# First of equal maxima: a rank and a second maximum, or a product with a constant matrix

## The chip, the cores and the metric

The kernel runs on one core of a Trainium2 chip. A core has a matrix engine (TensorE, in the profile PE, with its weight loads as PEld), a vector engine (VectorE, DVE), a scalar engine (ScalarE, ACT), a general engine (GpSimd, POOL) and DMA queues, most of them issued from SyncE (SP). The engines run side by side, each through its own instructions in order, and wait for each other by semaphores. TensorE writes its results to PSUM; the rest of the data lies in SBUF. The metric is device time in microseconds (us) from the first to the last instruction.

## The reference, cut to what matters

Routed attention over 4 batches, 8 heads, 768 positions and 64 channels, and then a dense block on the result. Each query and each key is assigned to one of 16 clusters, and a query attends only to keys of its own cluster.

```python
q_assign = np.argmax(np.einsum('bhsd,hcd->bhsc', q_n, c_n), axis=-1)   # q_n, k_n, c_n: normed
k_assign = np.argmax(np.einsum('bhsd,hcd->bhsc', k_n, c_n), axis=-1)
mask = q_assign[:, :, :, None] == k_assign[:, :, None, :]
scores = scale * np.matmul(q, k.transpose(0, 1, 3, 2))
scores = np.where(mask, scores, -1000000000.0)
scores = scores - np.max(scores, axis=-1, keepdims=True)
attn = np.exp(scores)
attn = attn / (np.sum(attn, axis=-1, keepdims=True) + 1e-09)
x = attn @ v                       # then (B,H,S,D) -> (B*S, H*D) = 3072 x 512
h = x @ w_in                       # 512 x 2048
sp = np.maximum(h, 0.0) + np.log1p(np.exp(-np.abs(h)))
return (h * erf(sp)) @ w_out       # 2048 x 512
```

`argmax` takes the first of equal maxima. That tie rule is what the change computes in another way. The weights arrive as 64-bit floats, and the kernel turns them into 32-bit ones itself; this "conversion" is integer work on VectorE, ScalarE and GpSimd.

## The kernel before

The kernel works on pairs of heads: 4 batches of 4 pairs, 16 pairs in all. Each pair is first *routed* (every query and key gets its cluster), then *shifted* (a maximum of the masked scores per query), then its scores, exponentials and attention values are computed in 12 units (two halves of the queries by six blocks of keys). For batch 0 this is done in 48 slots, one unit each, in the order of the program text. In the first-slot work of a pair, the routing of the next pair is already carried along. From slot 45 on, the dense block is mixed in, and after slot 48 the order of the instructions is no longer kept to the program text.

The mask is carried by the product itself. Beside the 64 channels, the tiles `qm` and `km` hold 32 rows with one entry per cluster: for the query 1 at its cluster and 0 elsewhere, for the key 0 at its cluster and a huge negative number elsewhere. Their product is then 0 where the clusters agree and huge and negative where not.

The routing, cut (`P` = 128, `D` = 64, `C` = 16, `HW` = 384, `Q` = 32, `BIG` = 2^60):

```python
def route(p):
    ...
    for nm in "qk":                               # step 1: inputs
        raw = rowp.tile([P, S], F32, name=nm + "T")
        ve.transpose(out=raw, in_=st.pop(nm).rearrange("p n t -> p (n t)"))
    load_qk(p + 1)
    yield
    psim = ps_x.tile([P, HW], F32, name="psim", tag="x")
    for g in range(4):                            # step 2: similarities
        te.matmul(psim[2 * C * g : 2 * C * (g + 1)], lhsT=ccT[:, p % HP], rhs=...)
    vectors("q")                                  # ScalarE: query channels to bf16
    yield
    sims = routep.tile([P, HW], F32, name="sims") # step 3: which ones are maxima
    ve.transpose(out=sims, in_=psim)
    sim = sims.rearrange("p (g c) -> p g c", c=C)
    ve.reduce_max(out=mx, in_=sim, axis=AX.X)
    ve.tensor_tensor(out=sim, in0=sim, in1=mx..., op=ALU.is_equal)
    yield
    vectors("k")                                  # step 4: key channels to bf16
    yield
    ve.tensor_tensor(out=sim, in0=sim, in1=rank..., op=ALU.mult)        # step 5
    ve.reduce_max(out=mr, in_=sim, axis=AX.X)
    hot = routep.tile([P, HW], BF16, name="hot")
    for r, op in ((slice(0, D), ALU.is_equal), (slice(D, P), ALU.subtract)):
        ve.tensor_tensor(out=hot[r]..., in0=sim[r], in1=mr[r]..., op=op)
    hotT = routep.tile([P, HW], BF16, name="hotT")
    ve.transpose(out=hotT, in_=hot)
    yield
    ...                                           # step 6: hotT to qm and km:
    ve.tensor_scalar_mul(out=low["q"][r, e, cols], in0=hotT[g], scalar1=own[g, e : e + 1])
    ae.copy(out=low["k"][r, e, cols], in_=hotT[g])                      # 4 of these
    ae.activation(out=dst, in_=src, func=ACT.Copy, scale=scale)         # 2, after them
    yield
```

The equality gives 1 for every maximum, so two equal ones both get a 1. The product with `rank` (16 for the first cluster, down to 1 for the last, times `BIG` in the key half) and a second maximum single out the first.

Shift, scores and sums, cut to what the text speaks of:

```python
sm = ps_x.tile([P, HW], F32, name="sm", tag="x")         # 24 per pair, two per step
te.matmul(sm, lhsT=st["qm"][...], rhs=st["km"][...])
ve.tensor_reduce(out=nmx[...], in_=sm, axis=AX.X, op=ALU.max, negate=True)
...
te.matmul(sc[...], lhsT=st["kT"]..., rhs=st["qT"]...)    # scores, float part
te.matmul(sc[...], lhsT=st["km"]..., rhs=st["qm"]...)    # scores, mask and shift
ae.activation(out=pr, in_=sc, func=ACT.Exp, scale=D**-0.5)
ge.tensor_tensor(out=acc, in0=..., in1=pr, op=ALU.add)   # sums of the exponentials
te.matmul(st["av", half]..., lhsT=st["v"][:, j, e], rhs=pr)
te.matmul(psum..., lhsT=minus, rhs=acc)                  # then den on VectorE, and xT
...
hp = ps_x.tile([P, GW, TB], F32, name="hp", tag="x")     # dense block, hidden
po = ps_x.tile([P, DM], F32, name="po", tag="x")         # dense block, output
```

The pool `ps_x` has four PSUM buffers for all of psim, sm, av, psum, hp and po. Each hidden and output tile is moved out of PSUM by VectorE (`g`, `osb`), and every finished hidden chunk goes through a gate of Softplus and Erf on ScalarE and products on GpSimd.

In the 48 slots, a table says how many steps of the current pair, of the next pair (ahead of and behind the scores), and of the conversion go into each of a pair's 12 slots.

Of the kernel before, what the change touches and what calls it, by code (L numbers as in the profile page):

```python
# [23 lines left out]
HW = S // 2  # L24
# [11 lines left out]
BIG = 2.0**60  # L36
# [30 lines left out]
def kernel(  # L67
# [24 lines left out]
    routep = pool("routep", 1)  # L92
# [7 lines left out]
    ps_x = pool("ps_x", 4, space=PSUM)  # L100
# [4 lines left out]
    rank = const.tile([P, C], F32, name="rank")  # L105
# [40 lines left out]
    def load_qk(p):  # L146
        load(p, "q", q, stage)
        load(p, "k", k, stage, nc.sync if p else nc.scalar)
# [12 lines left out]
            ge.memset(t["k"][e * D + SH : e * D + SH + 1, e], 1.0)  # L161
    for t in prs:
        ge.memset(t[:, :, HW : HW + 2], EPS)

# [85 lines left out]
    for it in range(2):  # L250
# [4 lines left out]
            out=twice, in0=ss, scalar=inv, in1=norm, op0=ALU.mult, op1=ALU.add  # L255
# [3 lines left out]
            out=norm, in0=twice, scalar1=0.5, scalar2=(1e-6 if it else 0.0),  # L259
            op0=ALU.mult, op1=ALU.add,  # L260
# [11 lines left out]
    def route(p):  # L272
        st = pairs[p]
        low = lows[p % 2]
        for e in range(2 if p > 1 else 0):
            r = e * D + SH
            nc.sync.dma_start(out=low["q"][r : r + 1, e], in_=low["q"][r + 1 : r + 2, e])
        for nm in "qk":
            raw = rowp.tile([P, S], F32, name=nm + "T")
            ve.transpose(out=raw, in_=st.pop(nm).rearrange("p n t -> p (n t)"))  # L280
            st[nm + "T"], st[nm + "m"] = raw, low[nm]
# [16 lines left out]

        vectors("q")
        yield  # L300

        sims = routep.tile([P, HW], F32, name="sims")
        ve.transpose(out=sims, in_=psim)
        n = HW // C
        sim = sims.rearrange("p (g c) -> p g c", c=C)
        mx = routep.tile([P, n], F32, name="mx")
        ve.reduce_max(out=mx, in_=sim, axis=AX.X)
        ve.tensor_tensor(
            out=sim, in0=sim, in1=mx.unsqueeze(2).to_broadcast([P, n, C]), op=ALU.is_equal
        )  # L310
        yield
        vectors("k")
        yield

        ve.tensor_tensor(
            out=sim, in0=sim, in1=rank.unsqueeze(1).to_broadcast([P, n, C]), op=ALU.mult
        )
        mr = routep.tile([P, n], F32, name="mr")
        ve.reduce_max(out=mr, in_=sim, axis=AX.X)

        hot = routep.tile([P, HW], BF16, name="hot")
        for r, op in ((slice(0, D), ALU.is_equal), (slice(D, P), ALU.subtract)):
            ve.tensor_tensor(
                out=hot[r].rearrange("p (g c) -> p g c", c=C), in0=sim[r],
                in1=mr[r].unsqueeze(2).to_broadcast([D, n, C]), op=op,
            )
        hotT = routep.tile([P, HW], BF16, name="hotT")
        ve.transpose(out=hotT, in_=hot)
        yield
        late = []  # L330
        for half in range(2):
            cols = slice(half * HW, (half + 1) * HW)
            for e in range(2):
                r = slice(e * D, e * D + Q)
                g = slice(half * Q, (half + 1) * Q)
                if half == 0:
                    ve.tensor_scalar_mul(out=low["q"][r, e, cols], in0=hotT[g], scalar1=own[g, e : e + 1])
                else:
                    late.append((low["q"][r, e, cols], hotT[g], own[g, e : e + 1]))
                g = slice(D + half * Q, D + (half + 1) * Q)  # L340
                ae.copy(out=low["k"][r, e, cols], in_=hotT[g])
        for dst, src, scale in late:
            ae.activation(out=dst, in_=src, func=ACT.Copy, scale=scale)
        yield


# [249 lines left out]
    def aside(p):  # L596
# [12 lines left out]
    def advance(p, n):  # L609
        for _ in range(n):  # L610
            next(ready[p])
# [12 lines left out]
    for c in range(C):  # L624
        ve.memset(rank[0:D, c : c + 1], float(C - c))
    ve.tensor_scalar_mul(out=rank[D:P], in0=rank[0:D], scalar1=BIG)
    ve.memset(alleps, S * EPS)
    for t in maxima:
        ve.memset(t, FLOOR)
# [50 lines left out]
    for u in range(2 * NJ * HP, len(units), 2):  # L680
        p, half, j = units[u]
# [59 lines left out]
```

## Time and profile before

| | before |
|---|---|
| median of 3 runs | 1228.26 us (1228.07 to 1229.61) |
| profiled execution | span 1227.4 us, mean granted TensorE clock 0.978 |
| hidden products `hp` | 384.4 us busy, 1536 records |
| output products `po` | 367.8 us busy, 768 records |
| maxima `nmx` | 195.4 us busy on VectorE, 384 instructions |
| exponentials `pr` | 147.4 us busy on ScalarE, 192 instructions |
| HBM read, written | 35.68 MB, 6.29 MB |

A page of the profile gives for each engine its busy time and share, then the span in 40 equal slices with the busy share in tenths, then the DMA queues, the chain of waits that ended last, and the costliest groups of instructions. A group's line reads: engine, operation, output from inputs by the names in the program, shapes, count, then busy time and the mean of one in ns, then how long the engine was idle just ahead of these instructions and which engine ended most of it. One float product counts as two records, because it takes two passes. Busy times can also be asked for any stretch of time, and waits as a list of who waited for whom: total, how often, longest.

In the chain of the whole span, TensorE has 74%, VectorE 11%, ScalarE 6%, DMA 2% and GpSimd 1%; 7% is time in which an engine waited for nothing that the profile shows.

### The profile page before, as it was taken

What the parts mean: (1) busy time and instruction counts of PE and PEld (TensorE: products, weight loads), DVE (VectorE), ACT (ScalarE), POOL (GpSimd) and SP (SyncE); (2) the same over time, 40 slices, a digit from 0 to 9 for tenths busy, and PEclk for the clock granted to TensorE, in tenths of its full rate; (3) what the DMA queues carried; (4) which work ended last, traced back from release to release, by engine and by line L of the source; (5) the groups of instructions that cost most, each with busy time, mean ns of one, the idle gap of its engine ahead of it and who ended that gap; (6) DMA issues with size and microseconds to landing.
All of it is one profiled execution on the core that took longest, in us unless ns stands there. A gap on an engine that the chain in (4) does not pass through costs nothing.

```text
span 1227.4 us, 13359 instructions
## 1 busy us (share of the span) xinstructions
PE 1158.3 (94%) x4897; PEld 618.2 (50%) x4897; DVE 541.5 (44%) x999; ACT 567.8 (46%) x675; POOL 465.8 (38%) x462
## 2 busy tenths in 40 slices
PE   4888879989999999999999999999999999999998
PEld 1222235554354445555456445556456456576663
DVE  6889885675444345334344344334435112011121
ACT  3656656647362647164364445356264254032222
POOL 2467764357332345244234144235234343030200
PEclk8889999889999999999999999999999999999999
DMA  7344323132020202010020201002000000000000
GB/s 134 77 105 104 81 82 84 41 103 33 16 48 9 39 9 39 9 35 13 10 48 1 48 10 27 21 10 39 4 27 1 9 9 1 12 6 17 1 18 18
DMA packets 140753, 42.95 MB, mean 35 GB/s; under 512 B 133520, under 2 KB 133520, under 8 KB 140688
## 3 DMA queue, kind: packets, MB, share of 16 engines
q1 hardware_dynamic: 137552, 41.70, 15.2%
q10 hardware_dynamic: 3136, 0.39, 0.3%
q8 instruction: 39, 0.64, 0.2%
q14 instruction: 26, 0.21, 0.1%
HBM read 35.68 MB, written 6.29 MB: 34 GB/s over the span
## 4 chain that ended last, share of the span: by engine, by line
PE 74%; DVE 11%; issue 7%; ACT 6%; DMA 2%; POOL 1%; SPq 0%; ACTq 0%; DVEq 0%
PE po L58 25%; PE hp L58 24%; PE sc L58 12%; PE av L58 7%; PE sm L58 4%; DVE nmx L58 3%; ACT L58 2%; DVE w_out L58 2%; DVE den L58 1%; DVE sims L58 1%; ACT inv L58 1%; PE psim L58 1%; PE psum L58 1%; ACT km L58 1%; ACT pr L58 1%
## 5 line engine op out<-in xcount | busy, mean ns | idle before, releaser
L58 PE MATMUL hp<-xT,w_in 128*128 128x256 f32 x1536 | 384.4, 387 | 4.1 <-DVE xT L58 2.4
L58 PE MATMUL po<-w_out,g 128*128 128x512 f32 x768 | 367.8, 597 | 0.6 <-DVE den L58 0.6
L58 POOL TENSOR_TENSOR acc<-acc,pr 128x384 f32<-128x384 f32 x256 | 240.3, 968 | 318.0 <-ACT pr L58 317.9
L58 PEld LDWEIGHTS hp<-xT,w_in 128*128 128x128 f32 x1536 | 287.2, 192 | 124.0 <-issue 79.8
L58 DVE TENSOR_REDUCE nmx<-sm 128x1 f32<-128x384 f32 x384 | 195.4, 551 | 144.9 <-PE sm L58 144.0
L58 ACT ACT_TABLE_LOAD x113 | 145.0, 1283 | 230.7 <-DVE g L58 128.8
L58 ACT ACTIVATE pr<-sc 128x768 f32<-128x768 f32 x192 | 147.4, 807 | 166.7 <-PE sc L58 166.4
L58 PEld LDWEIGHTS po<-w_out,g 128*128 128x128 f32 x768 | 141.8, 190 | 108.0 <-issue 95.0
L58 PE MATMUL sc<-qT,kT 64*128 64x384 f32 x768 | 185.3, 537 | 6.2 <-ACT pr L58 6.1
L58 POOL TENSOR_TENSOR g<-a_s,g 128x512 f32<-128x512 f32 x88 | 110.6, 1287 | 198.4 <-ACT a_s L58 198.4
L58 DVE COPY g<-hp 128x512 f32<-128x512 f32 x96 | 65.9, 687 | 257.1 <-PE hp L58 256.8
L58 PE MATMUL av<-pr,in_v 128*64 128x386 f32 x768 | 144.5, 505 | 2.5 <-DVE nmx L58 2.5
L58 PE MATMUL sm<-km,qm 128*128 128x384 bf16 x384 | 106.1, 342 | 31.3 <-DVE nmx L58 14.5
L58 PEld LDWEIGHTS sc<-qT,kT 64*128 64x128 f32 x768 | 70.9, 190 | 85.4 <-issue 45.6
L58 POOL TENSOR_TENSOR acc<-pr,pr 128x384 f32<-128x384 f32 x64 | 66.7, 1063 | 94.2 <-ACT pr L58 94.2
L58 PEld LDWEIGHTS av<-pr,in_v 128*64 128x64 f32 x768 | 50.0, 138 | 92.8 <-issue 78.7
L58 PEld LDWEIGHTS <-qm 128*128 128x128 bf16 x384 | 35.2, 99 | 99.6 <-issue 73.2
L58 DVE SCALAR_TENSOR_TENSOR den<-psum,inv 128x384 f32<-128x384 f32 x32 | 17.8, 557 | 145.5 <-ACT inv L58 145.1
L58 ACT ACTIVATE a_s<-a_s 128x2048 f32<-128x2048 f32 (+2 forms) x40 | 55.8, 1413 | 13.3 <-DMA a_s<-in_moe_w_out_dram 8.9
L58 PE MATMUL sc<-qm,km 64*128 64x384 bf16 x384 | 59.5, 329 | 1.9 <-DMA qm<-nmT 1.9
L58 ACT ACTIVATE a_s<-g 128x2048 f32<-128x2048 f32 x24 | 45.8, 1910 | 33.0 <-DVE g L58 31.8
L58 ACT COPY nmT<-pn 6x128 bf16<-6x128 bf16 x32 | 8.1, 252 | 98.3 <-PE pn L58 97.9
(66 smaller groups left out, 604.7 us busy)
## 6 DMA issues: line engine op xcount, KB each, us to landing
w_out<-in_moe_w_in_dram SPq DMA_DIRECT2D x16, 512.0 KB, 4.5
in_q<-in_q_dram SPq DMA_DIRECT2D x64, 96.0 KB, 3.0
in_v<-in_v_dram SPq DMA_DIRECT2D x32, 192.0 KB, 3.0
out_dram<-osb SPq DMA_DIRECT2D x24, 256.0 KB, 2.0
in_k<-in_k_dram SPq DMA_DIRECT2D x60, 96.0 KB, 3.3
a_s<-in_moe_w_out_dram SPq DMA_DIRECT2D x8, 512.0 KB, 3.4
w_out<-in_moe_w_out_dram SPq DMA_DIRECT2D x8, 512.0 KB, 4.3
qm<-nmT SPq DMA_DIRECT2D x192, 0.2 KB, 1.7
```

What stands on the lines that cost most here:

```text
L58: ins = getattr(self.engine, name)(*args, **kw)
```

## The change

It is meant to take vector work out of the routing. The equality now writes `hot` at once, as bf16, with a 1 at every maximum. After the transpose, a product with a constant 128x128 bf16 matrix `first` finds the first one: `first` has 1 on its diagonal and -1 wherever its row is an earlier cluster of the same group of 16. A result is then its own hot entry minus the number of hot entries before it: 1 at the first maximum, 0 or negative everywhere else. The query half is scaled by `own` and cut off at 0 on the way out of PSUM; the key half becomes `BIG` times the result minus `BIG`, which is 0 at the first maximum and at or below `-BIG` elsewhere. The results `won` lie in a buffer of `ps_x`, where `hotT` lay in SBUF.

```diff
+    ge.memset(first, -1.0)
+    for base, pattern, sign, op, fill in (
+        (-1, [[1, P]], -1, ALU.is_ge, 0.0),
+        (0, [[-C, P // C], [0, C]], 1, ALU.is_ge, 0.0),
+        (0, [[-1, P]], 1, ALU.not_equal, 1.0),
+    ):
+        ge.affine_select(out=first, in_=first, compare_op=op, fill=fill, ...)
...
         ve.reduce_max(out=mx, in_=sim, axis=AX.X)
+        hot = routep.tile([P, HW], BF16, name="hot")
         ve.tensor_tensor(
-            out=sim, in0=sim, in1=mx.unsqueeze(2).to_broadcast([P, n, C]), op=ALU.is_equal
+            out=hot.rearrange("p (g c) -> p g c", c=C), in0=sim,
+            in1=mx.unsqueeze(2).to_broadcast([P, n, C]), op=ALU.is_equal,
         )
-        yield
-        vectors("k")
-        yield
-
-        ve.tensor_tensor(out=sim, in0=sim, in1=rank..., op=ALU.mult)
-        mr = routep.tile([P, n], F32, name="mr")
-        ve.reduce_max(out=mr, in_=sim, axis=AX.X)
-        hot = routep.tile([P, HW], BF16, name="hot")
-        for r, op in ((slice(0, D), ALU.is_equal), (slice(D, P), ALU.subtract)):
-            ve.tensor_tensor(out=hot[r]..., in0=sim[r], in1=mr[r]..., op=op)
         hotT = routep.tile([P, HW], BF16, name="hotT")
         ve.transpose(out=hotT, in_=hot)
         yield
+        won = ps_x.tile([P, HW], F32, name="won", tag="x")
+        te.matmul(won, lhsT=first, rhs=hotT, start=True, stop=True)
+        yield
         for half in range(2):
             for e in range(2):
                 if half == 0:
-                    ve.tensor_scalar_mul(out=low["q"]..., in0=hotT[g], scalar1=own[g, e : e + 1])
+                    ve.tensor_scalar(
+                        out=low["q"]..., in0=won[g], scalar1=own[g, e : e + 1], scalar2=0.0,
+                        op0=ALU.mult, op1=ALU.max,
+                    )
                 else:
-                    late.append((low["q"]..., hotT[g], own[g, e : e + 1]))
+                    ae.activation(out=low["q"]..., in_=won[g], func=ACT.Relu, scale=own[g, e : e + 1])
-                ae.copy(out=low["k"]..., in_=hotT[g])
+                ae.activation(
+                    out=low["k"]..., in_=won[g], func=ACT.Identity, bias=nbig[g], scale=BIG
+                )
-        for dst, src, scale in late:
-            ae.activation(out=dst, in_=src, func=ACT.Copy, scale=scale)
         yield
+        vectors("k")
+        yield
...
     plan = (                       # own steps, next pair's before and behind, conversion
-        (1, 0, 1, 1), (1, 0, 2, 0), (1, 0, 2, 0), (1, 0, 1, 0), (0, 0, 0, 0), (0, 0, 2, 0),
-        (0, 0, 2, 1), (0, 0, 2, 1), (0, 1, 0, 3), (0, 0, 0, 3), (0, 0, 2, 1), (0, 0, 1, 2),
+        (1, 0, 1, 0), (1, 0, 2, 0), (1, 0, 2, 1), (1, 0, 1, 0), (0, 0, 1, 2), (0, 0, 2, 0),
+        (0, 0, 1, 2), (0, 0, 1, 2), (0, 1, 0, 2), (0, 1, 0, 0), (0, 0, 2, 1), (0, 0, 1, 2),
     )
...
         if r % NJ == 2 and slot > 2:
+            if after:
+                advance(p + 1, 1)
+                after -= 1
             part = divide(slot - 3)
             next(part)
```

The order of the steps in a pair becomes: inputs; similarities; maxima, `hot` and its transpose; the product; the copies to `qm` and `km`; the key channels to bf16. It is again six steps. In the plan by slots, the two steps of maxima that stood together in slots 6 and 7 are spread over slots 4 to 9, one or two at a time, and the conversion's twelve steps lie in other slots. In the slot where a half's sums are formed, the next pair's product comes ahead of them.

More of the change, by code (lines that the diff above doesn't have):

```diff
@@ L104 @@
     minus = const.tile([P, D], F32, name="minus")
-    rank = const.tile([P, C], F32, name="rank")
+    first = const.tile([P, P], BF16, name="first")
+    nbig = const.tile([P, 1], F32, name="nbig")
     ccT = const.tile([P, HP, 2 * C], F32, name="ccT")
@@ L163 @@
         ge.memset(t[:, :, HW : HW + 2], EPS)
+    ge.memset(first, -1.0)
[4 more added lines that the diff above has]
+    ):
+        ge.affine_select(
+            out=first, in_=first, compare_op=op, fill=fill, base=base, pattern=pattern,
+            channel_multiplier=sign,
+        )
     w_steps = []
@@ L307, in route @@
         ve.reduce_max(out=mx, in_=sim, axis=AX.X)
+        hot = routep.tile([P, HW], BF16, name="hot")
         ve.tensor_tensor(
-            out=sim, in0=sim, in1=mx.unsqueeze(2).to_broadcast([P, n, C]), op=ALU.is_equal
-        )
-        yield
-        vectors("k")
-        yield
-        ve.tensor_tensor(
-            out=sim, in0=sim, in1=rank.unsqueeze(1).to_broadcast([P, n, C]), op=ALU.mult
-        )
-        mr = routep.tile([P, n], F32, name="mr")
-        ve.reduce_max(out=mr, in_=sim, axis=AX.X)
-        hot = routep.tile([P, HW], BF16, name="hot")
-        for r, op in ((slice(0, D), ALU.is_equal), (slice(D, P), ALU.subtract)):
[L323 to L326, printed above, removed]
+            out=hot.rearrange("p (g c) -> p g c", c=C), in0=sim,
+            in1=mx.unsqueeze(2).to_broadcast([P, n, C]), op=ALU.is_equal,
+        )
         hotT = routep.tile([P, HW], BF16, name="hotT")
@@ L329, in route @@
         yield
-        late = []
+        won = ps_x.tile([P, HW], F32, name="won", tag="x")
+        te.matmul(won, lhsT=first, rhs=hotT, start=True, stop=True)
+        yield
         for half in range(2):
@@ L336, in route @@
                 if half == 0:
-                    ve.tensor_scalar_mul(out=low["q"][r, e, cols], in0=hotT[g], scalar1=own[g, e : e + 1])
-                else:
-                    late.append((low["q"][r, e, cols], hotT[g], own[g, e : e + 1]))
+                    ve.tensor_scalar(
+                        out=low["q"][r, e, cols], in0=won[g], scalar1=own[g, e : e + 1], scalar2=0.0,
+                        op0=ALU.mult, op1=ALU.max,
+                    )
+                else:
+                    ae.activation(
+                        out=low["q"][r, e, cols], in_=won[g], func=ACT.Relu, scale=own[g, e : e + 1]
+                    )
                 g = slice(D + half * Q, D + (half + 1) * Q)
-                ae.copy(out=low["k"][r, e, cols], in_=hotT[g])
-        for dst, src, scale in late:
-            ae.activation(out=dst, in_=src, func=ACT.Copy, scale=scale)
+                ae.activation(
+                    out=low["k"][r, e, cols], in_=won[g], func=ACT.Identity, bias=nbig[g], scale=BIG
+                )
+        yield
+        vectors("k")
         yield
@@ L623 @@
     ve.memset(minus, -1.0)
-    for c in range(C):
-        ve.memset(rank[0:D, c : c + 1], float(C - c))
-    ve.tensor_scalar_mul(out=rank[D:P], in0=rank[0:D], scalar1=BIG)
+    ve.memset(nbig, -BIG)
     ve.memset(alleps, S * EPS)
```

## The prediction

> **What bounds the kernel now.** I read the page first: busy time by engine, then its forty slices, to see whether one engine bounds the whole span.
>
> ```profile
> span 1227.4 us, 13359 instructions
> ...
> PE 1158.3 (94%) x4897; PEld 618.2 (50%) x4897; DVE 541.5 (44%) x999; ACT 567.8 (46%) x675; POOL 465.8 (38%) x462
> ...
> PE   4888879989999999999999999999999999999998
> ...
> DVE  6889885675444345334344344334435112011121
> ```
>
> There are two regimes. One slice is 30.7 us. In the first six or seven slices (batch 0, attention with almost no dense layer beside it) TensorE is not full and VectorE is at 8 to 9 tenths. From about 194 us on, TensorE is full and VectorE is at 3 to 5 tenths. The 44% of VectorE over the whole span describes neither. So I asked for busy times by stretch: three head pairs of the first regime, each from one pair's input transposes to the next one's, and the long middle.
>
> ```profile
> 34.50:71.40 36.90, 31.45 (x145) 9.59 (x144) 29.48 (x54) 22.58 (x36) 20.56 (x20) 0.84 0.44 103
> 71.40:107.70 36.30, 31.52 (x172) 10.30 (x172) 33.15 (x60) 23.97 (x37) 25.14 (x25) 1.00 0.39 92
> 107.70:145.00 37.30, 31.99 (x161) 9.88 (x160) 32.72 (x60) 23.59 (x38) 24.84 (x25) 0.95 0.37 89
> ```
> ```profile
> 330.00:1072.00 742.00, 733.81 (x3161) 398.86 (x3159) 277.43 (x514) 337.57 (x387) 263.78 (x264) 1.00 0.10 20
> ```
>
> The columns are length, then TensorE, weight loads, VectorE, ScalarE, GpSimd. In the first regime a pair takes 36 to 37 us, of which VectorE works about 33 and TensorE about 32: two nearly full engines in program order, each waiting for the other in turn. In the middle TensorE is busy 733.8 of 742 us (99%): only its own work counts there, and 8 us is all that removing waits could bring.
>
> The waits between 34.5 and 194 us say what the gaps are:
>
> ```profile
> DVE nmx L58 <- PE sm L58: 15.5, 13, 2.7
> ```
> ```profile
> PE sm L58 <- DVE nmx L58: 9.9, 12, 2.4
> ```
>
> The first is VectorE waiting for a score product before its maximum, the second a score product waiting for a PSUM buffer that a maximum has yet to free. They come from the bursts of four maxima in one slot.
>
> Last, the groups of VectorE in the same window, for the operations that the change touches:
>
> ```profile
> L58 DVE TENSOR_TENSOR hot<-sims,mr 64x384 bf16<-64x384 f32 x8 | 7.1, 884 | 0.2
> ...
> L58 DVE TENSOR_SCALAR qm<-hotT,own 32x384 bf16<-32x384 bf16 x8 | 4.9, 618 | 0.3
> L58 DVE TENSOR_TENSOR sims<-sims,mx 128x384 f32<-128x384 f32 x4 | 3.9, 984 | 0.1
> ...
> L58 DVE TENSOR_TENSOR sims<-sims,rank 128x384 f32<-128x384 f32 x4 | 3.5, 882 | 0.0
> ...
> L58 DVE TENSOR_REDUCE mr<-sims 128x24 f32<-128x384 f32 x4 | 2.2, 553 | 0.1
> ```
>
> The last numbers before the second bar are mean ns of one. The four operations that go (rank product, second maximum, two halves of hot) lie one after another in the chain of waits of this regime, with nothing of another engine between them.
>
> [...]
>
> **The change, part by part.** There are 16 pairs: pair 0 in the prologue, pairs 1 to 4 routed in the first regime, pairs 5 to 15 in the second.
>
> *Removed from VectorE, first regime, per pair:* 0.882 + 0.553 + 2 x 0.884 = 3.20 us. The equality stays, with a bf16 output; I leave it at 0.98. The two query copies on VectorE stay, from PSUM in place of SBUF: 2 x 0.62 before; I put 0.55 for each, as the maxima from PSUM (0.548) and the first denominator step (0.554) take, so 0.1 us is gained.
>
> *Added to VectorE:* the second query copy waits for ScalarE to finish its first key copy from the same tile. A 32x384 copy of ScalarE took 0.51 us, so VectorE idles about 0.6 us per pair. Net, VectorE is relieved of about 2.7 us in a period of 36.5.
>
> *What of it reaches the end:* VectorE works some 33 of 36.5 us and TensorE 32, so relief of VectorE alone is soon stopped by TensorE. I let three quarters through: 2.0 us per pair. *Spreading the maxima* removes part of the burst waits, 15.5 us over 4.3 periods = 3.6 us each; I take a quarter, 0.9 us. *The product* costs TensorE about 0.35 us per pair here (a score product of the same shape took 0.350). Sum: 2.0 + 0.9 - 0.35 = 2.5 us per pair, times 4 = **10 us gained in the first regime**. The conversion steps are the same twelve per pair, elsewhere in the slots.
>
> *Prologue (pair 0):* the chain sims, maximum, equality, rank product, second maximum, two halves, transpose, ScalarE copies ran without a gap. It loses 0.57 + 0.56 + 1.12 = 2.25 us of VectorE and gains about 0.4 us of product. But the two key casts (0.84 us each), which were hidden under VectorE, now come after the winner copies, and these alternate between VectorE and ScalarE for about 0.5 us more: 1.7 + 0.4 + 0.5 = 2.6 us back. **About 0.**
>
> *Second regime, 11 pairs:* the VectorE relief is worth nothing, and the product is new work for the bound. Two score products of its shape took 0.49 us together at 0.33 each, so one adds 0.16 us: 11 x 0.16 = 1.8 us. Then, TensorE takes its work in order, and the product stands in its queue soon after the similarities. For pair 8, before:
>
> ```profile
> 414.65 0.49 PE L58 MATMUL psim<-kT,ccT 128*32 128x384 f32 x2
> 415.08 0.70 PE L58 MATMUL hp<-xT,w_in 128*128 128x256 f32 x2
> 415.61 1.88 PE L58 MATMUL po<-w_out,g 128*128 128x512 f32 x4
> 417.33 0.59 PE L58 MATMUL hp<-xT,w_in 128*128 128x256 f32 x2
> ```
>
> The similarities end at 415.14. VectorE begins their transpose at 415.21, and its steps start 0.6 us apart (415.21, 415.83, 416.42, 417.01), so a fourth step, the transpose of hot, would end at 417.6: 2.45 us after the similarities. A dense product is two passes of 0.215 us (hp) or 0.43 us (po), so 0.43 or 0.86 us. In the built order of the changed kernel, what stands between similarities and winners for pairs 5 to 15 is between 2.1 us (four hp, one score) and 4.5 us, mostly 2.6 (six hp, three po, or two and two) or 3.4 (eight hp, or two po and four hp). Against 2.45 us plain, or 3.1 us where a dense eviction (0.68) falls between, or over 3.5 us where GpSimd stretches the equality (1.68 us at 298.5), TensorE waits 0 to 1 us. I take 0.3 us on average: 11 x 0.3 = 3.3 us. **Second regime: 1.8 + 3.3, about 5 us lost.**
>
> Sum: -10 + 0 + 5 = -5 us. I lean a little further, because the new plan by slots looks fitted to the new step lengths: 1228.3 - 7.3 = **1221 us**.
>
> **The rivals.** *First: TensorE pays for it.* The winners stay in one of only four PSUM buffers that hidden layer, output, attention values, sums and score products also use. Eight reads that partly alternate between engines hold it 4.5 us or more; where ScalarE is inside a gate (activations of 1.9 us, table loads of 1.28 us; at 557 us its copies took until 569) it is held 8 us or longer, and the sums product after the attention values then finds no buffer. Before, the copies came out of SBUF and held none. For it: one of those waits alone is 2 to 3 us of the bound. Against: most pairs have 4 us of attention products first, which cover the hold. It would make 1228 to 1235. *Second: the first regime is set by TensorE, not VectorE.* For it: its 32 busy us per period. Against: it waits for VectorE there, and the chain runs mostly over VectorE. Then 2 us per pair at most would be spread's, and the time 1226 to 1230. *Third: both engines loosen together*, because a removed VectorE operation also frees buffers earlier and shortens TensorE's waits: 4 us per pair, 1210 to 1213.
>
> **Range and chances.** First regime 4 to 17 us gained, second 2 to 12 us lost; the two extremes seldom meet: 1211 to 1231. Faster by over 2% means under 1203.7 us, 24.6 us less: and TensorE's gaps in the three periods shown are only 5.5, 4.8 and 5.3 us, so four periods hold some 21 us: 0.03. Slower by over 2% would need more than 3 us lost in each of the eleven later pairs, on top of the gain: 0.02.
>
> **What would show it.** In the first regime the period from one pair's input transposes to the next should be about 34 us in place of 36.5, with VectorE busy near 30 and its wait for score products under 15 us; the dense layer should begin about 10 us earlier. From there to the end it should take about 5 us longer, with winners' products waiting for the hot transpose by 3 us in sum. The prediction is wrong if the first-regime period stays above 36 (rival two), or if hidden, output or sums products wait for ScalarE by more than 5 us (rival one).

## The result, and the profile after

The changed kernel takes **1242.2 us** (median of 4 runs, 1241.8 to 1245.3). Against the kernel before, timed on the same chip, the ratio is 1.0114 with a 95% interval of 1.0095 to 1.0132: slower by 1.1%, where I had predicted 1221 us and a gain.

The page of the changed kernel, the lines that answer to those shown of before:

```profile
span 1240.1 us, 13300 instructions
...
PE 1167.3 (94%) x4913; PEld 622.6 (50%) x4913; DVE 496.1 (40%) x919; ACT 567.6 (46%) x673; POOL 463.5 (37%) x466
...
PE   3788969899999999999999999999999999999998
...
DVE  5578876554434244333334244343335112011121
...
PEclk8689999989999999999999999999999999999999
```

VectorE did lose work: 541.5 us busy before, 496.1 now. In most of the first ten slices it stands a tenth or more lower, but TensorE does not stand higher there. The last line is new to this text: it is the TensorE clock that was granted, and it has dips early in the run. The kernel before had such dips too:

```profile
PEclk8889999889999999999999999999999999999999
```

To see where the time went I use one milestone in all that follows: the product that sums the exponentials of one half of a pair (`psum`). There are 32, numbered 0 to 31; number 10 is the first of pair 5, where the routing is already in the later regime. Start times in the two traces:

| sums product | before | after | later by |
|---|---|---|---|
| 0 | 56.29 | 62.80 | 6.5 |
| 10 | 335.44 | 337.32 | 1.9 |
| 17 | 559.80 | 564.22 | 4.4 |
| 18 | 596.77 | 604.89 | 8.1 |
| 31 | 1029.86 | 1042.49 | 12.6 |

So the first part (up to number 10) gained nothing and lost 1.9 us; 6.5 us are already lost at number 0, and some of that comes back. The later part lost 10.7 us, and not evenly: 3.7 us of it between numbers 17 and 18. The spans differ by 12.7 us, so this is the whole loss.

**First part.** Busy time by stretch, one pair of the first regime, from its input transposes to the next pair's (columns: length, TensorE, weight loads, VectorE, ScalarE, GpSimd, then granted clock, DMA share, GB/s):

```profile
113.50:150.00 36.50, 32.54 (x164) 10.21 (x163) 28.75 (x55) 23.53 (x36) 24.76 (x25) 0.95 0.40 90
```

VectorE works 28.7 us per pair, some 4 less than before. The period is still 36.5 us. (From input transposes to input transposes, the first three periods are 42.8, 36.5 and 36.5 us; before they were 39.0, 36.3 and 37.3. The stretch of 36.9 us that the prediction shows first begins 2.2 us behind that pair's transposes.) VectorE now waits instead: for score products, between 34.5 and 194 us, 28.8 us in all where it was 15.5:

```profile
DVE nmx L58 <- PE sm L58: 28.8, 18, 4.9
```

TensorE's waits between 14 and 200 us show two that are new in size (before: 3.2 us for the first, none for the second):

```profile
PE sm L58 <- ACT km L58: 9.8, 4, 5.9
PE pn L58 <- DVE den L58: 8.4, 3, 2.8
```

Of the first, 6.2 us belong to pair 0. The second comes once in each of three pairs. The timeline of one, cut to the instructions that hand it on (start, duration, engine, operation; in brackets what the engine had waited for):

```profile
118.74 0.34 PE L58 MATMUL won<-hotT,first 128*128 128x384 bf16 x1 [0.24 <-DVE hotT L58]
119.27 0.87 PE L58 MATMUL psum<-acc,minus 128*64 128x384 f32 x4 [0.20 <-DVE nmx L58]
119.71 0.60 DVE L58 TENSOR_SCALAR qm<-won,own 32x384 bf16<-32x384 f32 x1
...
120.24 0.58 ACT L58 ACTIVATE inv<-psum,alleps 128x384 f32<-128x384 f32 x1 [0.84 <-PE psum L58]
...
121.40 0.57 ACT L58 ACTIVATE km<-won,nbig 32x384 bf16<-32x384 f32 x1
122.01 0.61 DVE L58 TENSOR_SCALAR qm<-won,own 32x384 bf16<-32x384 f32 x1 [1.70 <-ACT km L58]
...
122.99 0.55 DVE L58 SCALAR_TENSOR_TENSOR den<-psum,inv 128x384 f32<-128x384 f32 x1
...
123.59 0.22 PE L58 MATMUL pn<-identb,nm 128*6 128x128 bf16 x1 [2.81 <-DVE den L58]
...
124.75 1.56 PE L58 MATMUL av<-pr,in_v 128*64 128x386 f32 x4
```

Read from the bottom: TensorE waits 2.81 us for a PSUM buffer, which `den` frees. `den` stands in VectorE's queue behind the second query copy, that copy waits 1.70 us for ScalarE's first key copy of the same tile `won`, and that one stands behind the two `inv` steps. All this while `won`, sums and attention values hold the four buffers. Then a second cost: after the gap the attention product takes 1.56 us where the same four records took 0.85 us at 119.94. The granted clock in the stretch behind the gap is 0.59 (the last column but two of this row; it was 1.00 in the 6 us before):

```profile
124.00:128.00 4.00, 4.00 (x16) 1.10 (x14) 0.88 (x3) 3.90 (x7) 0.00 (x0) 0.59 0.01 0
```

**Later part.** ScalarE and VectorE around sums product 17 (564.22 us after, 559.80 before), first the changed kernel, then the kernel before:

```profile
563.04 1.91 ACT L58 ACTIVATE a_s<-a_s 128x2048 f32<-128x2048 f32 x1
...
567.32 0.57 ACT L58 ACTIVATE km<-won,nbig 32x384 bf16<-32x384 f32 x1
...
569.20 0.58 ACT L58 ACTIVATE inv<-psum,alleps 128x384 f32<-128x384 f32 x1
...
572.35 0.56 DVE L58 SCALAR_TENSOR_TENSOR den<-psum,inv 128x384 f32<-128x384 f32 x1 [2.78 <-ACT inv L58]
```
```profile
562.24 0.58 ACT L58 ACTIVATE inv<-psum,alleps 128x384 f32<-128x384 f32 x1
...
565.22 0.56 DVE L58 SCALAR_TENSOR_TENSOR den<-psum,inv 128x384 f32<-128x384 f32 x1 [7.37 <-ACT inv L58]
```

Five copies out of `won` (the last is at 567.32) now stand between the gate (`a_s`) and the logarithm of the sums (`inv`). The logarithm starts 5.0 us after the sums product, against 2.4 us before, and `den` 8.1 against 5.4. TensorE then waits 1.06 us for the attention output `xT` that `den` leads to (at 574.34 us), and the granted clock falls once more (0.57 between 575 and 579 us). Number 25 shows the same: the logarithm starts 5.0 us after the sums product, against 2.4 us before. From number 10 to number 31 TensorE is idle for 11.9 us in all, against 8.2 before.

### The profile page after: what moved, and what is told of

It reads as the page before. It is cut to its first block, busy times and chain, and to the rows that moved or that the text cites. A ratio compares the mean times of both kernels' runs of the same rounds, so it can differ in the third digit from the quotient of the medians.

```text
span 1240.1 us, 13300 instructions
## 1 busy us (share of the span) xinstructions
PE 1167.3 (94%) x4913; PEld 622.6 (50%) x4913; DVE 496.1 (40%) x919; ACT 567.6 (46%) x673; POOL 463.5 (37%) x466
## 4 chain that ended last, share of the span: by engine, by line
PE 62%; ACT 7%; issue 6%; DVE 3%; DMA 1%; POOL 0%; ACTq 0%; SPq 0%; DVEq 0%; POOLq 0%
PE po L58 24%; PE hp L58 21%; PE sc L58 9%; PE av L58 5%; PE sm L58 3%; ACT L58 2%; ACT a_s L58 2%; ACT km L58 1%; ACT inv L58 1%; PE psum L58 1%; DVE den L58 1%; DMA a_s<-in_moe_w_out_dram 1%; ACT pr L58 1%; PE psim L58 1%; ACT qm L58 1%
## 5 line engine op out<-in xcount | busy, mean ns | idle before, releaser
L58 PE MATMUL hp<-xT,w_in 128*128 128x256 f32 x1536 | 389.7, 390 | 10.4 <-DVE xT L58 6.8
L58 ACT ACTIVATE a_s<-a_s 128x2048 f32<-128x2048 f32 (+2 forms) x40 | 55.8, 1412 | 16.6 <-DMA a_s<-in_moe_w_out_dram 16.4
L58 ACT ACTIVATE km<-won,nbig 32x384 bf16<-32x384 f32 x64 | 36.6, 573 | 32.1 <-DVE qm L58 31.3
```

The lines of the kernel that those rows point to most:

```text
L58: ins = getattr(self.engine, name)(*args, **kw)
```

## The experiments

The first theory was my rival one: the result of the product is held in PSUM by readers on two engines that wait for one another. Its rivals: the product itself, the new order of steps (the copies one step earlier, the casts of the key channels one step behind them in place of two steps ahead), and the new plan. All runs in one table; the last two columns are from each run's trace, in us against the kernel before (positive is later): where sums product 10 starts, and what is lost from there to number 31.

| run | median us | ratio, 95% interval | to no. 10 | 10 to 31 |
|---|---|---|---|---|
| changed kernel | 1242.2 | 1.0114 [1.0095, 1.0132] | +1.9 | +10.7 |
| e1 result moved to SBUF | 1239.3 | 1.0094 [1.0064, 1.0123] | +1.2 | +11.6 |
| e2 no product | 1234.4 | 1.0063 [1.0042, 1.0084] | -11.9 | +12.4 |
| e3 rank, new plan | 1212.7 | 0.9886 [0.9866, 0.9906] | -16.4 | 0.0 |
| e4 product, old plan | 1247.3 | 1.0179 [1.0143, 1.0215] | +9.8 | +7.5 |
| e5 casts with the product | 1241.9 | 1.0100 [1.0065, 1.0134] | +3.1 | +10.9 |
| e7 e5, result in SBUF | 1229.9 | 1.0019 [1.0005, 1.0033] | -4.7 | +8.2 |
| e8 e5, no product | 1231.6 | 1.0028 [1.0010, 1.0047] | -13.9 | +18.4 |
| e9 e3, casts late | 1235.9 | 1.0066 [1.0045, 1.0087] | +8.8 | +1.6 |
| e11 old order, SBUF | 1208.6 | 0.9839 [0.9791, 0.9887] | -24.0 | +1.2 |
| e12 old order, no product | 1215.4 | 0.9890 [0.9849, 0.9930] | -25.1 | +13.5 |
| e13 e3, old conversion | 1230.7 | 1.0026 [1.0010, 1.0043] | -0.9 | +3.3 |
| e14 old order from pair 5 | 1238.8 | 1.0103 [1.0067, 1.0138] | -5.2 | +11.1 |
| e15 e12, late transpose | 1215.7 | 0.9895 [0.9866, 0.9924] | -24.1 | +13.5 |
| e16 e11 from pair 5 | 1230.8 | 1.0023 [1.0009, 1.0037] | +0.9 | -0.4 |
| e17 e11 up to pair 4 | 1218.3 | 0.9916 [0.9889, 0.9943] | -20.7 | +10.8 |

e2, e8, e12 and e15 leave the tie rule out: every maximum stays marked. The column up to number 10 comes from single executions and moves by some us from one to another: up to sums product 5, e14 and the changed kernel run the same program, and stand at +3.7 and +7.3, with a granted clock of 8 tenths and 6 tenths in the second fortieth of the span.

**e1: the result leaves PSUM by one copy**, at the head of the next step.

```diff
         te.matmul(won, lhsT=first, rhs=hotT, start=True, stop=True)
         yield
+        wonb = routep.tile([P, HW], BF16, name="wonb")
+        ve.tensor_copy(out=wonb, in_=won)      # all eight copies then read wonb
```

> The changed kernel, but the product's result is moved to SBUF (bf16) by one VectorE copy right after it, and the eight copies read that. It adds some 0.6 us of VectorE per pair and frees the PSUM buffer at once; the reads of the two engines no longer wait for one another. Theory A (the held PSUM buffer and the alternating reads take the gain): the 2.8 us wait of the transpose of the row maxima for a buffer, once per pair in the first regime, goes, and so do the cold stretches after it; about 1229 us (1225 to 1233). Theory B (ScalarE's order, the key casts after the copies, takes it): hardly any change, 1239 to 1242. Theory C (the new plan by slots takes it): no change, 1241 to 1243. Theory D (the product's own time on the full TensorE takes it): no change.

Measured: 0.2% less in the ratio, with overlapping intervals, and next to nothing gained in either part. The move does what it is for: `won` is held 0.9 to 1.5 us per pair in place of 5.2 to 9.6, and the waits of the row maxima's transposes for `den` are gone. So the hold by itself was not the whole cause. The wait of the first score product for the key copies and casts grew to 20.6 us between 14 and 200 us (9.8 in the changed kernel): ScalarE, not the buffer, was now in the way.

**e2: no product**, the copies read `hotT` (tie rule left out), all else as changed.

```diff
-        won = ps_x.tile([P, HW], F32, name="won", tag="x")
-        te.matmul(won, lhsT=first, rhs=hotT, start=True, stop=True)
```

> The changed kernel without the product: the copies read the transposed hot tile itself, so that all of several equal maxima count (the tie rule is left out). It shows what taking away the vector operations is worth alone, with the changed plan and step order. Theory A: the lost time comes back and part of the relief shows, 1222 to 1228 us. Theory B or C: it stays at 1238 to 1242, for the casts and the plan are as in the changed kernel. Theory D: some 3 to 6 us below the changed kernel.

Measured: still slower than before by 0.6%, with four vector instructions less and nothing put in their place. The later part loses 12.4 us with no product in it. So order or plan costs by itself.

**e3: the kernel before with the new plan; e4: the changed kernel with the old plan.** Each swaps the table of slots and the early step ahead of the sums.

> The kernel before (rank and second maximum) with the new plan by slots and the step moved ahead of the sums: the plan alone. Theory C: the plan itself costs, 1236 to 1243 us. Theories A and B: within 4 us of the kernel before, and if the spread of the maxima does what it is for, 1223 to 1228.

> The changed kernel's routing with the plan by slots of the kernel before: the product alone. Theory A: the winners' copies now come after the sums, so the buffers are as short, and it stays at 1237 to 1244 us. Theory B: the first maxima come a slot later than in the new plan, so the casts are done in time: 1233 to 1238. Theory C: 1228 to 1232.

Measured: the plan alone makes the kernel before 1.1% **faster**, all of it before sums product 10, and nothing is lost later. The old plan makes the changed kernel slower still. The plan is acquitted; what remains is the order of the steps and the product.

**e13: which column of the plan.** e3 with the maxima spread as in the new plan, the conversion's twelve steps where they were.

```diff
-        (1, 0, 1, 0), (1, 0, 2, 0), (1, 0, 2, 1), (1, 0, 1, 0), (0, 0, 1, 2), (0, 0, 2, 0),
-        (0, 0, 1, 2), (0, 0, 1, 2), (0, 1, 0, 2), (0, 1, 0, 0), (0, 0, 2, 1), (0, 0, 1, 2),
+        (1, 0, 1, 1), (1, 0, 2, 0), (1, 0, 2, 0), (1, 0, 1, 0), (0, 0, 1, 0), (0, 0, 2, 0),
+        (0, 0, 1, 1), (0, 0, 1, 1), (0, 1, 0, 3), (0, 1, 0, 3), (0, 0, 2, 1), (0, 0, 1, 2),
```

> The kernel with rank and new plan, with the conversion's steps put back into the slots of the old plan: the spread of the maxima alone. If the spread is what gained 1.1%, ratio 0.987 to 0.991; if the conversion's new places gained it, 0.996 to 1.004. My guess is that the spread gives two thirds: 0.991 to 0.994.

Measured: 1.0026. Spread maxima alone gain nothing; with them in place, the conversion's new places are worth the step from 1.0026 to 0.9886, about 17 us. The new places with the old maxima were not run, so the two may need each other.

**e5, e7, e8: casts of the key channels ahead of the copies again**, in the same step as the product, e7 with the move to SBUF too, e8 without the product.

```diff
         te.matmul(won, lhsT=first, rhs=hotT, start=True, stop=True)
+        vectors("k")
         yield
...
-        vectors("k")
         yield
```

> The changed kernel with one line moved: the two key casts on ScalarE stand with the product, ahead of the winners' copies, as they did in the kernel before. Theory B (the casts behind the copies hold up the first maxima of a pair): the waits of score products for ScalarE's key tiles fall from 9.8 us (more in the kernel with the SBUF copy: 20.6) to under 4, the prologue is 1.5 to 2 us shorter, and the time is 1225 to 1232 us. Theory A (the held buffer and the alternating reads): at most 2 to 4 us less than the changed kernel, 1238 to 1240, with the 2.8 us waits of the transposes of row maxima still there.

> Both mendings at once: casts ahead of the copies, and the product's result moved to SBUF by one VectorE copy. If A and B each hold one half of the loss (the copy alone gave only 3 us because the late casts then stood in the way), it lies clearly under both single mendings: 1214 to 1224 us. If B alone matters, it equals the kernel with the early casts within 3 us. Against the kernel before it should be faster, for the plan alone gave 1.1%.

> No product (the copies read the transposed hot tile, the tie rule is left out) and the casts ahead of the copies: the vector operations taken away, with nothing put in their place. Against the kernel with the rank and the new plan (ratio 0.9886 to the kernel before) this shows what the four vector operations were worth. If VectorE bounds the first regime: 10 us or more below it, ratio 0.977 to 0.981. If latency and TensorE bound it: the same within 4 us, ratio 0.985 to 0.991.

Measured: e5 is as slow as the changed kernel: TensorE's waits for the key tile fall from 9.8 to 5.9 us, but those of the row maxima's transposes for `den` are still there (10.2 us between 14 and 200 us). e7 stands below e1 (1.0019 against 1.0094), so the place of the casts matters once the buffer is free, but it still only draws level with the kernel before. In these three, the plan's slot of two steps takes casts (1.68 us) and copies (six of 0.57 us) of ScalarE together, and a later step stands empty. So they did not test the old order cleanly. e9 and e11 come closer to it.

**e9: the old chain with the casts late**: e3, with `vectors("k")` moved behind the copies, into the same step (in the changed kernel they have a step of their own behind them).

```diff
-        vectors("k")                # step 4
         yield
...
+        vectors("k")                # step 6, behind the copies
         yield
```

> The kernel with the rank and the new plan (ratio 0.9886 to the kernel before), and only the two key casts moved behind the winners' copies. Theory B: they cost 8 to 20 us here too, ratio 0.995 to 1.005, with new waits of score products for ScalarE. Theory A: under 3 us, ratio 0.987 to 0.991.

Measured: 1.0066 against 0.9886 for e3. Moving two casts costs 1.8%, about 22 us, nearly all in the first part, with no product in the kernel: late casts can cost this much by themselves. The waits of TensorE for the key tile between 14 and 200 us, e9 first, then e3:

```profile
PE sm L58 <- ACT km L58: 27.4, 10, 6.2
```
```profile
PE sm L58 <- ACT km L58: 7.6, 6, 2.5
```

The first maxima need `km` whole: copies and casts. In e9 ScalarE does both in one stretch, 5 us long, with the next score product waiting at its end. In the changed kernel this happens in the first two pairs alone (9.8 us in sum); the later ones wait for `den`, as shown above.

**e11: the order of the kernel before, with the product and the move to SBUF.** Casts at step 4, product and move at step 5, copies at step 6.

```diff
         ve.transpose(out=hotT, in_=hot)
         yield
+        vectors("k")
+        yield
...
         te.matmul(won, lhsT=first, rhs=hotT, start=True, stop=True)
+        wonb = routep.tile([P, HW], BF16, name="wonb")
+        ve.tensor_copy(out=wonb, in_=won)
         yield
...                                 # copies from wonb
         yield
-        vectors("k")
-        yield
```

> The changed kernel with the steps of a pair in the order of the kernel before: equality and hot transpose in step 3, key casts in step 4, product and its move to SBUF in step 5, copies to qm and km in step 6. In the second regime the copies then come after the logarithm of the sums on ScalarE, as before, and not ahead of it. Theory E (the copies, made ready earlier, went ahead of the logarithm and so held the sums' and attention buffers): the steps of 4, 2 and 2 us that the changed kernel loses at pairs 10, 13 and 14 go; from the sums of pair 5 to the end it loses under 4 us against the kernel before, and the time is 1213 to 1222. Theory A or B alone: the second regime still loses 8 us or more, 1226 to 1232.

Measured: **1208.6 us, ratio 0.9839 [0.9791, 0.9887]**: faster than the kernel before and than the changed kernel, with nothing left out, and below the 1213 to 1222 that I had expected. Against e3, the rank in the same plan, the intervals overlap: that the product beats the rank is not shown. The granted clock by slices of its profiled execution (span 1204.6 us), and the stretch from 36 to 180 us, e11 first, then the changed kernel:

```profile
PEclk9999999999999999999999999999999999999999
```
```profile
36.00:180.00 144.00, 131.11 (x666) 48.33 (x663) 128.83 (x229) 96.72 (x150) 107.40 (x100) 0.99 0.43 104
```
```profile
36.00:180.00 144.00, 124.98 (x603) 38.76 (x603) 106.28 (x200) 90.53 (x140) 90.00 (x87) 0.91 0.38 88
```

In the same 144 us, e11 gets 666 matmul records done against 603, and at a clock of 0.99 against 0.91. VectorE is busier (128.8 us), because more work is put through; the wait of the row maxima's transpose for `den` is gone. The period of a pair is 32.3 us, and TensorE is busy for 31.2 of it. The move to SBUF costs one instruction of 0.55 us per pair, and the copies on VectorE then take 0.31 us each in the median in place of 0.60. The old order without the move was not run for the first part, so there the two are not told apart.

**e12: e11 without product and move** (tie rule left out).

> The same step order without the product (the copies read the transposed hot tile, the tie rule is left out): four vector operations less than the kernel with rank and new plan (ratio 0.9886 to the kernel before), and nothing else different but the place of the hot transpose. Theory E: no steps in the second regime, ratio 0.983 to 0.990. If it is near 1.003 as with the casts early, the step order is not what costs, and something in the hot tile's earlier place is. If VectorE were the bound of the first regime: 0.975 to 0.981.

Measured: level with e11 up to number 10, then 13.5 us lost. That was unexpected: less work, and a slower later part, as in e2 and e8.

**e14: the changed kernel, with the old order of steps from pair 5 on only**, `won` still read from PSUM.

> The changed kernel as it is for pairs 0 to 4; from pair 5 on only the casts of the maxima are at step 4, the product with the constant matrix at step 5 and the copies of its result (read from PSUM, no move to SBUF) at step 6, as the kernel before has its copies. Nothing is left out. Theory order (in the later part of the run the copies stand at step 5 ahead of the exponentials and logarithm that the next pair's sums product waits for; that order costs the later part): the 10.7 us that the changed kernel loses between the sums products of half 10 and half 31 fall to 2 to 4 us, time 1233 to 1236. Rival (the result of the product held in PSUM by alternating readers costs the later part, wherever the copies stand): still 8 us or more lost there, time 1240 to 1243.

Measured: my theory fell. The later part still loses 11.1 us. At sums product 17 the logarithm is back in its place, and the step from 17 to 18 falls from 3.7 to 1.4 us; other steps take over. `won` is now held 12.5 to 13.9 us in four of the later pairs, and 5.2 to 7.1 in the others. One of them, at number 21, in e14:

```profile
697.97 0.33 PE L58 MATMUL won<-hotT,first 128*128 128x384 bf16 x1
698.22 4.11 PE L58 MATMUL av<-pr,in_v 128*64 128x386 f32 x24
698.33 0.60 DVE L58 TENSOR_SCALAR qm<-won,own 32x384 bf16<-32x384 f32 x1 [2.25 <-PE won L58]
698.97 0.57 ACT L58 ACTIVATE km<-won,nbig 32x384 bf16<-32x384 f32 x1 [7.84 <-DVE qm L58]
699.58 0.61 DVE L58 TENSOR_SCALAR qm<-won,own 32x384 bf16<-32x384 f32 x1 [0.64 <-ACT km L58]
...
702.57 0.57 ACT L58 ACTIVATE km<-won,nbig 32x384 bf16<-32x384 f32 x1
703.24 0.87 PE L58 MATMUL psum<-acc,minus 128*64 128x384 f32 x4
```

The last read of `won` ends at 703.14 and the sums product starts at 703.24: `won` was held 5.2 us, longer than the 4.1 us of attention products that I had counted on to cover it. The trace names no wait for this buffer; the 0.1 us between the two argues for it. So the rival theory, the hold, fits the later part here.

**e16 and e17: the two parts apart.** e16 is the changed kernel up to pair 4 and e11 from pair 5 on; e17 is the reverse.

```diff
+        if p > 4:                   # e16; e17 has p <= 4
+            vectors("k")            # and the move to wonb, and no casts at the end
+            yield
```

> The changed kernel as it is for pairs 0 to 4; from pair 5 on the step order of the kernel before (casts at step 4, product at step 5, copies at step 6) and the move of the product's result to SBUF. Nothing is left out. Theory (in the later part both are needed, late copies and a short hold of the PSUM buffer; the step order alone kept an 11 us loss): loss between half 10 and half 31 falls from 10.7 to 1 to 3 us, time 1230 to 1234. Rival (the loss of the later part comes from the state that the earlier part leaves, whatever the order): still 8 us or more, 1238 to 1243.

> The mirror image: pairs 0 to 4 in the step order of the kernel before with the move to SBUF, pairs from 5 on as the changed kernel. Nothing is left out. Theory: the two parts add up, so the first part gains as in the run with both (24 us at half 10 against the kernel before) and the later part loses 10 to 11 us: time 1217 to 1221. Rival (the parts depend on one another): outside 1213 to 1225.

Measured: close to what the theory had. e16 loses nothing in the later part, e17 loses 10.8 us there, and its first part is 20.7 us ahead at number 10. By the medians, undoing the later part is worth 11.4 us (changed kernel to e16) or 9.7 (e17 to e11); undoing the first part is worth 23.9 (changed kernel to e17) or 22.2 (e16 to e11). The parts are separate and add up. In the later part neither the order alone (e14, 11.1 lost) nor the move alone (e1, 11.6) helps; both together leave 1.2 us or less. Late casts by themselves, or the product's own time, are not the cause there: e9 has the casts late and loses 1.6, and e11 and e16 have the product.

**e15: e12 with the transpose of the marks moved to step 5**, so that the copies' input is not ready long before.

> The tie rule is left out as in the run without the product in the old order (copies read the transposed vectors), with one edit: the transpose of the vectors is moved from step 3 to step 5, just ahead of the copies at step 6. Theory (in the later part, where the queues are ordered ahead of time by estimates and not by the program's order, the loss comes from copies whose input is ready early, so that they are set ahead of the exponentials and logarithms): the 13.5 us that the run without the product lost between the sums products of half 10 and half 31 fall to under 3 us, and the time from 1215.4 to about 1204 to 1207. Rival (the later part loses whenever the four vector instructions of the rank are gone, since the other work shifts): still 10 us or more lost there, time 1213 to 1217.

Measured: the theory behind it fell; 13.5 us were lost as in e12. ScalarE before sums product 17 (which starts at 541.7 us in e15):

```profile
536.24 1.23 ACT L58 ACTIVATE km<-hotT,nbig 32x384 bf16<-32x384 bf16 x2 [4.57 <-DVE hotT L58]
...
538.78 1.91 ACT L58 ACTIVATE a_s<-g 128x2048 f32<-128x2048 f32 x1
...
545.87 0.58 ACT L58 ACTIVATE inv<-psum,alleps 128x384 f32<-128x384 f32 x1
```

Two key copies stand ahead of the gate here; in e11 the gate's first step comes first. The logarithm starts 4.2 us after the sums product, in e11 2.1 us. So again copies are in front of the gate and the logarithm, and with no `won` in the kernel no hold can be the reason. Why the queue of the later part, which doesn't follow the text of the program, comes out this way without the product is not settled; moving the transpose did not change it.

## Why the prediction was wrong

- **"Relief of VectorE ... I let three quarters through: 2.0 us per pair."** This is the step that failed. In the changed kernel the periods are 42.8, 36.5 and 36.5 us where they were 39.0, 36.3 and 37.3: VectorE works 4 us less per pair and waits about as much longer, and TensorE waits 9.8 us for the key tile and 8.4 us for a buffer that `den` frees. My range of 4 to 17 us gained in this part did not hold either. The size of the relief need not have been the error. In the old order of steps, e11 is 7.6 us ahead of e3 at sums product 10 (-24.0 against -16.4), and e17, the same program as e11 up to pair 4, is 4.3 us ahead; my sum for relief less product had 6.6 (4 x (2.0 - 0.35)). These are single executions, so the agreement may be luck. What failed is that I took the new order for free. I wrote that it "is again six steps" and priced instructions, not who waits behind them. With the order of before and the move to SBUF in pairs 0 to 4 alone (e17), the changed kernel is 23.9 us faster; and e9 shows that two casts of 0.84 us, moved behind the copies, can cost 22 us.
- **"Prologue: about 0."** It lost 1.9 us up to the first maximum of scores (23.86 us after, 21.93 before); the first score product starts 4.0 us later and the first sums product 6.5. The transpose of the marks starts 2.1 us earlier (14.30), as worked out. But all copies and casts then lie in a row until 22.3 us, and the first score product waits 5.87 us for `km`. I had 0.5 us for the alternation; the two engines take turns from 15.78 to 18.3 us.
- **"Spreading the maxima ... 0.9 us per pair."** Wrong in both cause and size: the spread alone gains nothing (e13); the conversion's new places, which I had called "the same twelve per pair, elsewhere in the slots", gain 17 us on top of it.
- **"Second regime: 1.8 + 3.3, about 5 us lost."** It lost 10.7, inside my range of 2 to 12 but not for my reasons. The 1.8 us for the products is about right: e11, with the product and few new waits, loses 1.2, and e16 gains 0.4. The 3.3 us of waits for the transpose of the marks did not come: the trace has 2.1 us of them (`won` for `hotT`), all in the first 200 us. In their place the logarithm of the sums comes late where copies stand between it and the gate (5.0 against 2.4 us at numbers 17 and 25), and where it is in its place, in e14, the hold of `won` fits, which I had only as rival one. How the two divide the loss stays open, since e12 and e15 lose 13.5 us with no `won` at all.
- **"Most pairs have 4 us of attention products first, which cover the hold."** The hold of `won` was 5.2 to 9.6 us in the later pairs of the changed kernel.
- **My own signs.** Rival two was to show in a first-regime period above 36 us. The period is 36.5, but rival two is not what happened: TensorE waits there for ScalarE's `km` and for buffers, and e11 brings the period to 32.3. Rival one was to show in waits of hidden, output or sums products for ScalarE above 5 us; they are 0.9 us in the whole run, though the hold is real: the wait shows on other tiles (`pn` for `den`, gone in e1). The signs told that a step was wrong, not which.
- **The clock** was in no step. One less the mean granted clock, times the span, is 27.0 us before (clock 0.978), 34.7 in the changed kernel (0.972), 12.1 in e3 (0.990) and 4.8 in e11 (0.996). These are not us of time: in 46 timed runs of the kernel before on one chip, with clocks from 0.972 to 0.989, a straight line gives some 0.3 us of time for each us lost in this way (an estimate, with much scatter). And some 10 us of it, before and after, lie in one stretch from 19 to about 40 us (granted clock 0.50 from 20 to 39 us before, and from 20 to 42 after) that the executions of e3 and e11 do not have (9 tenths or more there in e3, 1.00 in e11). So of the 36 us between the spans of the changed kernel and e11 the clock is a part, of unknown size. The gap at 120.8 us was paid twice: as a wait of 2.81 us, and again behind it, where attention records that had taken 0.85 us took 1.56.

## What to carry to other kernels

When a change shortens a chain, list for each engine's queue what now stands in front of what, and price the order as well as the instructions; two casts that moved behind the copies that the next product needs cost more here (22 us, e9) than the shorter chain was to gain (10 us). For a result in a scarce PSUM buffer with readers on two engines, try moving it to SBUF by one instruction; here that paid only once the readers also came at a time when nobody waited behind them (e1 and e7 against e11). Test a change with several parts in both directions: here the plan was a gain, the order a loss, and their sum looked like a product that doesn't pay.

## What the runs showed of the hardware

- **The clock after a gap.** TensorE stands still from 120.8 to 123.6 us in the changed kernel, 2.8 us. The granted clock is 1.00 in the 6 us up to 124 us, then 0.85 from 124 to 125, 0.50 from 125 to 128 and 0.97 from 128 to 130, and four attention records take 1.56 us behind the gap in place of 0.85 ahead of it. The other two waits of 2.81 us for `den` end at 87.1 and 161.4 us, and behind them the clock is 0.50 from 88 to 90 us and from 163 to 165. Not every gap is followed by this: in the kernel before, TensorE stands still from 177.6 to 180.0 us, and the clock is 1.00 from 180 to 186.
- **Two readers of one PSUM tile.** In these programs they take turns: 0.64, 0.61 and 0.64 us from one start to the next in e14, though the two never read the same rows: VectorE reads the first 32, ScalarE the others. Each start but the first follows a wait that the other engine's instruction ended (the last two 0.64 and 0.68 us long), so it is the program that orders them. The copies out of SBUF in the kernel before are not ordered so: one of each engine starts at 557.20 us.
- **Sizes.** A 32x384 query copy on VectorE took 0.60 us on average from PSUM; from SBUF in bf16 it took 0.31 us in the median but up to 1.27, and 0.57 on average (e11); on ScalarE a key copy took 0.57 us from PSUM and 0.61 from SBUF. The equality with a bf16 output took 0.67 us on average between 34 and 194 us, where I had left 0.98. In the kernel before, the equality took 0.56 us in the ten pairs where no GpSimd instruction ran beside it, and 0.58 to 1.68 in the six where one did; with the bf16 output it took 0.54 to 0.56 and 0.56 to 1.56, again ten pairs and six.
